# Loading the first weight matrix behind the row loads of the first batch, and stage 1 of the second batch one step later

## The chip, the cores and the metric

The kernel runs on one core of a Trainium2 chip. The metric is device time in microseconds (us) of one launch; each time given is the median of several runs. The engines are PE (matmuls; PEld is its weight loads), DVE and ACT (elementwise work and copies), POOL (a slower elementwise engine that also issues one of the two DMA queues) and SP (which issues the other). Each engine works through its own instructions in the order in which the program lists them, and waits on semaphores for the others and for DMAs.

## The reference

The input x has 8 batches of 3136 rows of 256 features. A filter is applied along the rows by an FFT, a product and an inverse FFT. Then a low-rank mix over the rows is added, and a two-layer MLP over the features with a residual:

```python
X = np.fft.rfft(x, axis=1)
y = np.fft.irfft(X * (filt_r + 1j * filt_i)[None], n=3136, axis=1)
h = y.transpose(0, 2, 1) @ U @ V              # rank 32
u = y + h.transpose(0, 2, 1)
out = u + np.maximum(u @ w_ch1, 0.0) @ w_ch2  # 256 -> 1024 -> 256
```

## The kernel before

3136 is 49 times 64, so each transform is done in two matmul stages. The work on one batch b goes through these generators, each of which issues a small piece and then yields:

- `f1(b)`, or `f1_turned(b)` for batches 0 and 1: stage 1. A batch of x is loaded by `load_x(b, c)` (L127) in four chunks c, with POOL issuing the DMA and the DMA casting to 16 bits. Stage 1 of a chunk is four pieces of four matmuls (L282, tile pf), each copied out of PSUM by a pair of copies on ACT or DVE (L288, L290, tile t).
- `mid(b)`: the second forward stage, the filter and the first inverse stage. For batches 0 and 1 `turn` transposes stage 1's result on PE (L308, tile pt) and copies it (L310, tile a), half on DVE and half on ACT. Then come matmuls (L383, tile pz), the product with the filter on DVE (L391, tile uv; L395 and L396 combine its halves) and matmuls again (L344, tile pe), which ACT copies to e (L354).
- `ct` and `eb`: each e is written to DRAM (tile ct, L363) and read back by `load_e2` (L415) in another order as rows of eb. A batch has three parts of 16, 16 and 12 rows of four, and each part is read in two halves, h = 0 (columns r below 32) and h = 1. Two last rows of frequencies of batch 0 go to eb directly (L358). SP issues ct and the reads of eb, in the order of the program.
- `rank(b)` writes the low-rank term into the first 32 rows of eb (L437, on DVE).
- `s4(b)`: the last inverse stage (L455, tile pu), whose result ut feeds the MLP.
- The MLP goes over 49 groups of 512 rows, eight steps for each group. A step does `mm1` (L487, weights w1sb, tile phh, a relu on ACT, L490) for its own group and `mm2` (L510, weights w2sb, tile pc; a residual, L502, on each second step) for the group before. DVE copies pc to och (L517), and POOL issues the store (L522).

Batch 0 runs through all of its stages ahead of the first step; `unread` issues matmuls that nothing reads. From then on `plan` holds, for each of the steps, which generators of the later batches move on by one piece behind that step's mm1 and mm2. `deal(gen, count, a, z)` spreads count pieces evenly over the steps a to z. In the first 48 steps batch 1 gets its stage 1 (the last twelve pieces, as four are done ahead), its mid, its rank and its s4.

The change touches two places. One is what POOL does between filters and steps. In its queue the program lists, one behind another: filters, V, constants, chunk 0 of batch 1, w1 (L553), copies of the filters, two direct rows of eb, and then this block:

```python
for h in range(2):
    for p in (32, 64):
        nc.gpsimd.tensor_copy(seen[p:p + 32], eb[p:p + 32, 8 + 32 * h, 0:4])
    for c in ((1,), (2, 3))[h]:
        load_x(1, c)
nc.gpsimd.dma_start(w2sb, ...)
```

Nothing uses `seen` (L580). The copies read one column of a half of eb, so that POOL waits until that half of the rows has landed, and the loads listed after them are issued after that. The other place is the two lines of the plan for mid and stage 1 of batch 1.

Of the kernel before, what the change touches and what calls it, by code (L numbers as in the profile page):

```python
# [79 lines left out]
def kernel(  # L80
# [11 lines left out]
    nc = tc.nc  # L92
# [22 lines left out]
    def dram(t, off, dims):  # L115
        return bass.AP(tensor=t, offset=off, ap=[list(d) for d in dims])
# [7 lines left out]
    def load_x(b, c):  # L124
        t = sb.tile([98, 8 * DM], F16, tag="x", bufs=4, name="x")
        for a, n in ((0, 96), (96, 2)) if b == 0 else ((0, 98),):
            nc.gpsimd.dma_start(t[a:a + n], dram(x.tensor, (b * SEQ + 8 * c + 32 * a) * DM, [[32 * DM, n], [1, 8 * DM]]))  # L127
        xt[b, c] = t
# [30 lines left out]
    def spread_filters(i):  # L159
        s = slice(PARTS[i], PARTS[i + 1])  # L160
        copies = ((nc.vector.tensor_copy, nc.scalar.copy), (nc.vector.tensor_copy, nc.scalar.copy),
                  (nc.gpsimd.tensor_copy, nc.gpsimd.tensor_copy))[i]

        for s in (slice(PARTS[2], 19), slice(19, NK)) if i == 2 else (s,):
            for f, copy in enumerate(copies):
                copy(fab[64:128, f, s, :], fab[0:64, f, s, :])
# [12 lines left out]
    w1sb = cst.tile([128, 2, NH], F16)  # L179
# [5 lines left out]
    eb = cst.tile([97, NR, DM], F16)  # L185
# [11 lines left out]
    seen = cst.tile([128, 4], F16)  # L197
# [42 lines left out]
    def f1(b):  # L240
        for c in range(4):
            t = xt[b, c].rearrange("p (j d) -> p j d", d=DM)
            asb = sb.tile([98, 8, DM], F16, tag="asb", bufs=4, name="asb")
            for half in range(2):
                for i in range(2):
                    pf = bank("z", "pf")
                    for s in range(2):
                        j = 4 * half + 2 * i + s
                        nc.tensor.matmul(pf[0:98, 256 * s:256 * s + 256],  # L249
                                         ws[:, (8 * c + j) * 98:(8 * c + j + 1) * 98], t[:, j, :],  # L250
                                         start=(s == 0), stop=True, skip_group_check=True)
                    dst = asb[:, 4 * half + 2 * i:4 * half + 2 * i + 2, :]
                    src = pf[0:98].rearrange("p (j d) -> p j d", d=DM)
                    nc.scalar.copy(dst, src)  # L254
                    if half and i:
                        nc.sync.dma_start(dram(ct1[b], 8 * c * 96 * DM, [[DM, 96], [96 * DM, 8], [1, DM]]), asb[0:96])
                        nc.sync.dma_start(dram(ct0[b], 8 * c * DM, [[32 * DM, 2], [1, 8 * DM]]),
                                          asb[96:98].rearrange("p j d -> p (j d)"))
                    yield
# [8 lines left out]
    def f1_turned(b):  # L268
        t1[b] = (sb.tile([128, 2, 24, 128], F16, tag="ut", bufs=2, name="t1"),
                 sb.tile([128, 2, NR], F16, tag="t10", bufs=1, name="t10"))  # L270
        for c in range(4):
            t = xt[b, c].rearrange("p (j d) -> p j d", d=DM)
            for n in range(4):
                half, dh = n // 2, n % 2
                pf = bank("z" if b else ("z", "m", "z", "o")[n], "pf")
                if b == 0:

                    unread(pf, 2 if (c, n) == (3, 0) else 0)
                    unread(pf, 1, 120)
                for s in range(4):  # L280
                    j = 4 * half + s
                    nc.tensor.matmul(pf[:, 98 * s:98 * s + 98], t[:, j, 128 * dh:128 * dh + 128],  # L282
                                     ws[:, (8 * c + j) * 98:(8 * c + j + 1) * 98],
                                     start=(s == 0), stop=True, skip_group_check=True)
                j = 8 * c + 4 * half

                copy = nc.vector.tensor_copy if dh and not (b and c < 1) else nc.scalar.copy
                copy(t1[b][0][:, dh, :, 4 * j:4 * j + 16].rearrange("p k (j c) -> p k j c", c=4),  # L288
                     view(pf, 0, [[1, 24], [98, 4], [24, 4]]))
                copy(view(t1[b][1], NR * dh + j, [[1, 4], [32, 2]]), view(pf, 96, [[98, 4], [1, 2]]))  # L290
                yield
# [236 lines left out]
    def deal(gen, count, a, z):  # L528
        for i in range(count):
            plan[max(0, int(a + i * (z - a) / count))].append(gen)  # L530

    def later_x(b, c):
        load_x(b, c)
        yield

    f1s = [f1(b) if b > 1 else f1_turned(b) for b in range(NB)]
    mids = [mid(0, "o")] + [mid(b) for b in range(1, NB)]
# [12 lines left out]
        next(f1s[0])  # L550
    nc.gpsimd.dma_start(sv[32:97], sv_d.rearrange("k (r q) -> k r q", q=NQ))
    load_x(1, 0)
    nc.gpsimd.dma_start(w1sb, moe_w_ch1.rearrange("(h dd) c -> dd h c", h=2))  # L553
    spread_filters(2)
    v_rows(nc.gpsimd.tensor_copy, 0, 32)
    for i in range(13):
# [18 lines left out]
            next(f1s[1])  # L575
        unread(pw, 1)

    for h in range(2):
        for p in (32, 64):
            nc.gpsimd.tensor_copy(seen[p:p + 32], eb[p:p + 32, 8 + 32 * h, 0:4])  # L580
        for c in ((1,), (2, 3))[h]:
            load_x(1, c)
    nc.gpsimd.dma_start(w2sb, moe_w_ch2.rearrange("(t cc) e -> cc t e", t=8))
    for _ in s4s[0]:
        pass
# [1 line left out]
    def loads(b, part):  # L587
        load_e2(b, part)
        yield

    for b in range(1, NB):
        a, z = S[b - 1], S[b]
        e = z - (17 if b == 1 else 20 if b < 6 else 22)
        deal(mids[b], 13, a + {1: 8, 2: -3}.get(b, -5), e - 4)
        deal(mids[b], 4, e - 4, e)
        for p, at in enumerate((e - 5, e - 4, e + 1)):
            plan[at].append(loads(b, p))
        deal(ranks[b], 6, e, e + 6)
        deal(s4s[b], 16, e + 8, z - 2)
        if b == 1:  # L600
            deal(f1s[1], 12, 1, 8)
        if b + 1 < NB:
            for c in range(4):
                plan[a + (9 + 2 * c if b == 1 else 1 + 4 * c)].append(later_x(b + 1, c))
            deal(f1s[b + 1], 16, a + (21 if b == 1 else 10), z - (13 if b == 1 else 20))
# [40 lines left out]
```

## Time and profile before

| | |
|---|---|
| median of 3 runs | 520.44 us (519.37 to 521.15) |
| the profiled execution: its own time | 522.24 us |
| its span, first to last instruction | 520.5 us |
| granted clock of PE, mean | 0.993 |
| busy: PE, DVE, ACT, POOL | 497.2, 352.3, 377.1, 80.7 us |
| moved by DMA | 88.22 MB |

Times in the profile are counted from the first instruction of the span. In a line of the timeline the columns are start, duration, engine, line, operation, out<-in, and in brackets the idle time before it and what ended that. A line of the chain gives start, duration and what it was. A window gives its bounds and length, busy time of the engines with the number of instructions, PE's granted clock, the share of the DMA engines' time that was busy, and GB/s. A landing is counted from the issue of the DMA.

### The profile page before, as it was taken

To read this page: it belongs to the slowest core of one execution; us is meant where nothing else is said; L and a number is where in the kernel's file an instruction comes from. 1 tells how busy PE (TensorE), PEld (TensorE's weight loads), DVE (VectorE), ACT (ScalarE), POOL (GpSimd) and SP (SyncE) were. 2 spreads that over 40 slices of the span, in tenths; PEclk is the share of its full clock that TensorE was granted. 3 is DMA by queue.
4 is the path that set the end of the run, shared out by engine and by line. 5 is a ranking of instruction groups with operands and counts; after the bars stand their busy time and mean duration, and the time that the engine had idled before them with its cause. 6 is when DMAs were issued, how large, how long until landed. Compare 5 with 4: busy or idle time off the path is not lost.

```text
span 520.5 us, 11966 instructions
## 1 busy us (share of the span) xinstructions
PE 497.2 (96%) x4852; PEld 355.4 (68%) x4852; DVE 352.3 (68%) x469; ACT 377.1 (72%) x704; POOL 80.7 (15%) x122
## 2 busy tenths in 40 slices
PE   4887899999999999999999999899999999999997
PEld 4545556776767776777767777577667766776665
DVE  5886698588847974788747974689745995621112
ACT  6875779767985789668976799467985677666662
POOL 6662010111010120111010110012010010101110
PEclk9998999999999999999999999899999999999999
DMA  8997846758685586828684597618875136212113
GB/s 194 179 216 175 151 110 188 234 198 171 181 265 206 117 222 207 273 87 185 180 275 180 130 236 218 239 42 196 235 232 199 62 134 189 107 42 83 81 42 122
DMA packets 67375, 88.22 MB, mean 170 GB/s; under 512 B 4835, under 2 KB 51875, under 8 KB 67320
## 3 DMA queue, kind: packets, MB, share of 16 engines
q0 software_dynamic: 14704, 41.58, 30.8%
q1 hardware_dynamic: 52616, 45.88, 28.8%
q8 instruction: 38, 0.62, 0.5%
q14 instruction: 17, 0.14, 0.1%
HBM read 55.20 MB, written 47.78 MB: 198 GB/s over the span
## 4 chain that ended last, share of the span: by engine, by line
PE 82%; DMA 8%; DVE 4%; ACT 2%; issue 1%; POOL 1%; SPq 0%; POOLq 0%; DVEq 0%; ACTq 0%
PE pc L510 31%; PE phh L487 30%; PE pu L455 5%; PE pc L502 4%; PE pf L249 4%; PE pe L344 4%; PE pz L383 3%; DVE uv L391 2%; DMA ct<-e 2%; DMA w2sb<-in_moe_w_ch_dram 2%; DMA x<-in_x_dram 2%; DMA eb<-ct 2%; PE ph L422 1%; DMA fab<-in_filt_i_dram 1%; POOL x L127 1%
## 5 line engine op out<-in xcount | busy, mean ns | idle before, releaser
L490 ACT ACTIVATE h<-phh 128x512 f16<-128x512 f32 x392 | 235.9, 603 | 90.3 <-PE phh L487 88.8
L510 PE MATMUL pc<-w2sb,h 128*128 128x256 f16 x1568 | 234.9, 273 | 0.4 <-DMA w2sb<-in_moe_w_ch_dram 0.4
L487 PE MATMUL phh<-ut,w1sb 128*128 128x512 f16 (+7 forms) x896 | 233.9, 353 | 0.4 <-DVE ut L462 0.4
L510 PEld LDWEIGHTS <-h 128*128 128x128 f16 x1568 | 151.7, 97 | 91.8 <-issue 1.5
L517 DVE COPY och<-pc 128x512 f32<-128x512 f32 x98 | 67.6, 690 | 99.5 <-PE pc L502 98.2
L391 DVE TENSOR_TENSOR uv<-pz,fab 128x1024 f16<-128x1024 f32 (+1 forms) x104 | 120.8, 1179 | 12.6 <-PE pz L383 10.4
L522 POOL DMA_DIRECT2D out_dram<-och x48 | 39.0, 813 | 408.2 <-DVE och L517 392.5
L487 PEld LDWEIGHTS <-w1sb 128*128 128x128 f16 x896 | 77.5, 97 | 19.2 <-issue 1.5
L354 ACT CAST e<-pe 128x512 f16<-128x512 f32 x96 | 56.5, 591 | 19.4 <-PE pe L344 18.8
L462 DVE CAST ut<-pu 128x392 f16<-128x392 f32 x92 | 48.8, 560 | 23.8 <-PE pu L455 22.2
L254 ACT CAST asb<-pf 98x512 f16<-98x512 f32 x96 | 57.2, 598 | 0.2
L502 PE MATMUL pc<-idn,ut 128*128 128x128 f16 (+1 forms) x400 | 54.2, 220 | 0.0
L437 DVE COPY eb<-h 32x4096 f16<-32x4096 f16 x32 | 38.2, 1232 | 14.2 <-ACT h L434 14.1
L455 PE MATMUL pu<-sv,eb 97*128 97x49 f16 x1024 | 40.8, 188 | 4.8 <-DMA eb<-ct 4.8
L344 PE MATMUL pe<-uv,m 128*128 128x512 f16 (+1 forms) x117 | 41.3, 371 | 2.4 <-DVE uv L391 1.3
L455 PEld LDWEIGHTS <-eb 97*128 97x128 f16 x1024 | 37.8, 98 | 6.2 <-DVE eb L437 3.1
L502 PEld LDWEIGHTS <-ut 128*128 128x128 f16 (+1 forms) x400 | 38.2, 98 | 5.4 <-issue 0.8
L383 PE MATMUL pz<-a,m 128*128 128x512 f16 x96 | 36.2, 379 | 1.1 <-DVE a L310 1.0
L249 PE MATMUL pf<-x,ws 98*98 98x256 f16 x192 | 36.7, 273 | 0.0
L395 DVE TENSOR_TENSOR uv<-uv 64x1024 f16<-64x1024 f16 (+1 forms) x49 | 30.9, 630 | 1.7
L396 DVE TENSOR_TENSOR uv<-uv 64x1024 f16<-64x1024 f16 (+1 forms) x49 | 30.8, 628 | 0.7
L249 PEld LDWEIGHTS <-ws 98*98 98x98 f16 x192 | 22.4, 125 | 9.1 <-issue 0.4
(78 smaller groups left out, 225.8 us busy)
## 6 DMA issues: line engine op xcount, KB each, us to landing
out_dram<-och POOLq DMA_DIRECT2D x48, 512.0 KB, 3.8
ct<-e SPq DMA_DIRECT2D x47, 256.0 KB
eb<-ct SPq DMA_DIRECT2D x46, 256.0 KB
x<-in_x_dram POOLq DMA_DIRECT2D x28, 392.0 KB, 7.8
ct<-asb SPq DMA_DIRECT2D x24, 384.0 KB
a<-ct SPq DMA_DIRECT2D x18, 512.0 KB
x<-in_x_dram POOLq DMA_DIRECT2D x4, 384.0 KB, 8.0
ws<-ws SPq DMA_DIRECT2D x1, 600.2 KB
```

The costliest lines, as they stand in the source:

```text
L249: nc.tensor.matmul(pf[0:98, 256 * s:256 * s + 256], ws[:, (8 * c + j) * 98:(8 * c + j + 1) * 98], t[:, j, :], start=(s == 0), stop=True, s ...
L254: nc.scalar.copy(dst, src)
L344: nc.tensor.matmul(pe[:, 0:n], w, uv[:, f, o:o + n], start=(f == 0), stop=(b > 0 or f == 1))
L354: nc.scalar.copy(t[:, 2 * (i % 2):2 * (i % 2) + 2, :].rearrange("p k d -> p (k d)"), pe)
L383: nc.tensor.matmul(pz, a2m, src[:, k:k + 2, :].rearrange("p k d -> p (k d)"), start=True, stop=True)
L391: nc.vector.tensor_mul(uv[:, :, o:o + n], zin, fin)
L455: nc.tensor.matmul(pu[:, NQ * i:NQ * i + NQ], eb[:, 8 * n + i, d], sv[:, 8 * g + i, :], start=(i == 0), stop=True, skip_group_check=True)
L487: nc.tensor.matmul(ph[:, o:o + n], w1sb[:, dh, 128 * t:128 * t + 128], utv(b)[:, dh, t0:t0 + n], start=(dh == 0), stop=(dh == 1), skip_gro ...
L490: nc.scalar.activation(h, ph, RELU)
L502: nc.tensor.matmul(d, w, idn, start=False, stop=(dh == 1), skip_group_check=True)
L510: nc.tensor.matmul(o, gr.h[tt][:, 128 * i:128 * i + 128], w2sb[:, tt, :], start=(tt == 0), stop=False, skip_group_check=True)
L517: nc.vector.tensor_copy(gr.och[:, i - 1:i + 1, :], gr.pc.rearrange("p (j d) -> p j d", d=DM))
```

## The change

w1 is no longer issued behind chunk 0 of batch 1. It is issued behind a new copy into seen of two rows, 32 and 33, at column 8; these belong to the first halves of parts 0 and 1. The other copies and the loads of chunks 1 to 3 and w2 keep their order and now follow w1. The twelve pieces of stage 1 of batch 1 are dealt over steps 2 to 9 in place of 1 to 8 (the bound at the end is left out), and mid of batch 1 starts at step 9 in place of 8; the step at which its thirteen pieces end stays.

```diff
     load_x(1, 0)
-    nc.gpsimd.dma_start(w1sb, moe_w_ch1.rearrange("(h dd) c -> dd h c", h=2))
     spread_filters(2)
...
-    for h in range(2):
-        for p in (32, 64):
-            nc.gpsimd.tensor_copy(seen[p:p + 32], eb[p:p + 32, 8 + 32 * h, 0:4])
-        for c in ((1,), (2, 3))[h]:
-            load_x(1, c)
+    for parts, r in ((((32, 34),), 8), (((32, 64), (64, 96)), 8), (((32, 64), (64, 96)), 40)):
+        for p, q in parts:
+            nc.gpsimd.tensor_copy(seen[p:q], eb[p:q, r, 0:4])
+        if len(parts) == 1:
+            nc.gpsimd.dma_start(w1sb, moe_w_ch1.rearrange("(h dd) c -> dd h c", h=2))
+        else:
+            for c in (1,) if r == 8 else (2, 3):
+                load_x(1, c)
     nc.gpsimd.dma_start(w2sb, moe_w_ch2.rearrange("(t cc) e -> cc t e", t=8))
...
-        deal(mids[b], 13, a + {1: 8, 2: -3}.get(b, -5), e - 4)
+        deal(mids[b], 13, a + {1: 9, 2: -3}.get(b, -5), e - 4)
...
-            deal(f1s[1], 12, 1, 8)
+            deal(f1s[1], 12, 2, 9)
```

## The prediction

> **What bounds the kernel now.** I read the page first (busy shares, chain), then the chain between 30 and 80 us, the SP queue and its waits, the windows of the DMA engines, and the timeline of PE and DVE.
>
> ```profile
> PE 497.2 (96%) x4852; PEld 355.4 (68%) x4852; DVE 352.3 (68%) x469; ACT 377.1 (72%) x704; POOL 80.7 (15%) x122
> PE 82%; DMA 8%; DVE 4%; ACT 2%; issue 1%; POOL 1%; SPq 0%; POOLq 0%; DVEq 0%; ACTq 0%
> ```
>
> PE fills the span, so a change here counts only by the time PE loses before the stretch from about 76 us on, where it is busy without a break (16.00 of 16.00 us in the window 76 to 92). The chain says who holds PE before that:
>
> ```profile
> 36.14 3.45 DMA ct<-e
> 41.98 3.88 DMA eb<-ct
> 47.65 10.36 DMA w2sb<-in_moe_w_ch_dram
> 59.13 0.70 DVE a L310
> 75.17 0.70 DVE a L310
> ```
>
> Three stretches: the rows of batch 0 (ct written, read back into eb), then loads up to w2 at 58.01, then DVE. The SP queue and its waits:
>
> ```profile
> 27.00 5.02 SPq L363 DMA_DIRECT2D ct<-e  x3
> 34.81 0.59 SPq L415 DMA_DIRECT2D eb<-ct  x1
> 39.65 3.13 SPq L415 DMA_DIRECT2D eb<-ct  x4
> SPq L415 <- DMA ct<-e: 3.8, 3, 1.9
> ```
>
> The first read of rows (34.81) waits for ct writes issued by 27.4, some 7 us before. A later write took 3.45 us (first line of the chain above). The early ones ran beside w1, whose entry is
>
> ```profile
> L553 POOL DMA_DIRECT2D w1sb<-in_moe_w_ch_dram x1: 1005/1005/1005, 20.6 to 20.6; - x1
> DMA to landing us min/median/max: 12.9/12.9/12.9
> ```
>
> so it was in flight from 20.6 to 33.5. This is what the change can win. The windows of the loads (the second last number is the share of the DMA engines):
>
> ```profile
> 45.00:58.00 13.00, 10.47 (x165) 7.41 (x162) 7.21 (x18) 10.41 (x27) 3.98 (x8) 0.92 1.00 165
> 40.00:45.00 5.00, 2.18 (x52) 1.97 (x51) 3.43 (x6) 0.97 (x2) 0.94 (x3) 0.87 0.68 202
> ```
>
> From 45 to 58 the DMA engines are full: x chunks 1 to 3 release PE at 50.50, 53.27 and 55.42, w2 at 58.05. From 40 to 45 a third of them is free. Last, PE and DVE after that:
>
> ```profile
> 58.05 0.60 PE L510 MATMUL pc<-w2sb,h 128*128 128x256 f16 x4 [0.42 <-DMA w2sb<-in_moe_w_ch_dram]
> 60.09 0.59 PE L487 MATMUL phh<-ut,w1sb 128*128 128x512 f16 x2
> 60.29 2.42 DVE L391 TENSOR_TENSOR uv<-pz,fab 128x1024 f16<-128x1024 f32 x2 [0.47 <-PE pz L383]
> 75.91 0.38 PE L383 MATMUL pz<-a,m 128*128 128x512 f16 x1 [0.70 <-DVE a L310]
> ```
>
> DVE starts on batch 1 at 59.13, right behind the transposes at 58.49, and from 60.29 to its copy that ends at 75.86 no gap is over 0.05 us; PE then waits 0.70 us for that copy. So from 58 to 76 the time is DVE's start plus a fixed 16.7 us of work.
>
> **Part 1: w1 leaves 20.64.** POOL loses an issue of 1.0 us there. It gains nothing by it: its next work, a filter copy at 23.68, waited 2.0 us for a DMA. x chunk 0 of batch 1 stands ahead of w1 in the same queue. DVE multiplies back to back from 21.5 to 34.6, so that stage does not shorten. What moves is SP. If the early ct writes land by 32, the first row read goes at 32.1, when SP is free, in place of 34.81. The two ct writes behind it then leave at their results (ACT ends them at 33.66 and 34.79), not at 35.5 and 36.1. The reads of the third part need the last of them: 34.83 + 3.45 = 38.3, or 37.5 if it lands faster (SP issues the two direct rows up to then: result at 36.21 plus 1.20). Today they start at 39.65. So the rows gain 1.3 to 2.1 us; at worst nothing, if the writes were slow for another reason. I take 1.7: PE starts on the rows at 41.3 rather than 43.06. Its clock was 0.50 from 44 to 47, behind the idle gap; with a gap of 1.1 us it may stay at 1.00. Neither helps by itself, as PE waits for x at 50.50 anyway.
>
> **Part 2: w1 comes back behind the first halves of parts 0 and 1.** POOL waits with a two-row copy (0.18 us), then issues w1 (1.0 us). Queued behind it are the other copies into seen, x chunks 1 to 3 and w2, and PE waits for all of these loads. POOL was idle from 37.6 to 42.97, so the instructions hide if it is released by 41. The read of part 1 would leave SP at 35.4 (36.67 today). The third read let POOL go 3.3 us after its issue (39.65 to 42.97), so w1's issue comes at 39 at the earliest and 42 if nothing gets faster; I take 39.5 to 40.5, and bytes from 41 on.
>
> Its cost on the DMA engines: w2, of the same 512 KB, took from 55.42 to 58.05, 2.6 us; x at its best 2.15 us for 392 KB, which makes 2.8. I take 2.6, its own size and kind. Today the engines' work from 40 to w2 is 5.0 x 0.68 + 13.0 x 1.00 = 16.4 us. Add 2.6; take off the row traffic that now falls ahead of 40, 1.7 x 0.65 = 1.1 (the share between 40 and 41); 17.9 is left. At a share of 0.7 until 41 and 1.0 after it w2 lands at 41 + 17.2 = 58.2, **0.2 us later**. The bounds are wide. If w1 takes on the slow start of the stream (chunk 1 needed 6.8 us from its issue, against 2.15 between later chunks) w2 could land up to 2.8 us earlier; there ACT is the floor (seven relus of 0.60 and five pairs of copies of 0.68 come before it: 7.6 us from 47.5, so 55.1). If w1 starts at 42 and nothing overlaps, it is 2.6 to 2.9 us later. I stay near the middle because the free share from 40 to 45 (5 x 0.32 = 1.6 us) and the earlier rows about pay for 2.6.
>
> The first use of w1, at 49.10 today, then comes at about 48; w1 lands between 46 and 48.5. A wait there is hidden as long as x and w2 are later, and they are.
>
> The Trainium skill speaks against this part: in "DMA: Bandwidth & Descriptors", section "Rules for kernel authors", it says to issue a DMA early and wait on its semaphore late. By it w1 at 20.64, landed 15 us ahead of its use, is free where it stands, and the sum would be the late rival below. The trace agrees with half of that: w1 made no one wait at its use, but SP waited 3.8 us for writes that ran beside it.
>
> **Part 3: stage 1 a step later.** The twelve pieces of f1 go from steps 1 to 7 to steps 2 to 8; they issue no DMA, only four matmuls and a pair of copies each. So mid of batch 1 starts at step 9. Its SP writes move with it; SP's queue is empty from 42.8 to 68.1, so nothing waits there. Today w2's arrival is followed by one mm2 (0.44 us) and the transposes. Afterwards it is followed by that mm2, the last f1 piece (0.35), mm1 of step 9 (0.43), its mm2 (0.44) and residual (0.11), and then the transposes. DVE starts **1.3 us later** against w2. The work between the first and the third copy of a on DVE is the same and in nearly the same order, so the 16.7 us stay. PE does more in between: it waits longer for DVE but has one step (0.87) more behind it, so at that point the loss is 0.4. But two steps on the matmul of L344 at 80.32 follows DVE's add at 80.26, and there the full 1.3 comes back. Bounds: 0.4 and 1.3; I take 1.3, as that row is a direct handover.
>
> **Sum.** +0.2 + 1.3 = +1.5 us. The profiled execution took 522.24 us, 520.5 span and 1.7 around it; the next would take 523.7. The runs' median is 520.44, 1.8 below the profiled one, so I forecast **521.9**. 0.3% is 1.56 us, about what a measurement of this kernel can tell from no change.
>
> **Rivals.**
> - *w1 late* (slower). If the rows come no sooner, w1 is issued at 42, and x and w2 queue behind 2.6 us more: w2 at 60.6 to 60.9, and with the 1.3 it makes +3.9 to +4.2; half of that delay +2.6. For it: 45 to 58 is full already, and the row reads also wait for results of ACT at 36.21. Against: 3.8 us of SP waits on ct. It decides when the two-row copy runs after 41. About 523.9; chance 0.20.
> - *w1 fits in, and DVE's step is absorbed* (faster). The slow start falls on w1, w2 lands at 55.2 at ACT's floor (-2.8), and only 0.4 of DVE's step is left: -2.4, 518.0. For it: the free third from 40 to 45, and rows up to 2.1 us early. Against: L344's direct handover. Chance 0.22.
> - *A draw.* The stream gains 1.3 us and DVE's step takes it: 520.4. Chance 0.13.
> - The forecast, +0.7 to +2.3: chance 0.45, of which 0.26 lies over 0.3%.
>
> Slower 0.20 + 0.26 = 0.46; same 0.19 + 0.13 = 0.32; faster 0.22. The range runs from inside the fast rival to the middle of the late one, 518.2 to 523.9, and leaves out about half of each.
>
> **What would show it.** The first row read at about 32, the four at 37.5 to 38.5, the two-row copy at 39 to 40.5: part 1 right. w2 releasing PE at 58.2: part 2. DVE's first copy at 60.6 and PE's wait for the third at about 77: part 3. A two-row copy after 41.5 is the late rival; w2 before 56.5, or DVE's start not 1.8 us or more behind it, the fast one.

## The result, and the profile after

The changed kernel took **520.9 us** (median of 22 runs, 518.87 to 524.03), the kernel before 519.5 beside it (22 runs, 517.31 to 524.22); the ratio is 1.0033, with a 95% interval of 1.0017 to 1.0049. That is 0.9 to 2.5 us slower. The forecast was 521.9, in a range of 518.2 to 523.9.

The first view of the profile after is the timeline of the SP queue, with the SP queue's waits below it (engine, line and what it waited for: sum in us, times, longest).

```profile
32.19 0.58 SPq L415 DMA_DIRECT2D eb<-ct  x1
33.76 1.49 SPq L363 DMA_DIRECT2D ct<-e  x2
37.54 2.98 SPq L415 DMA_DIRECT2D eb<-ct  x4
...
SPq L363 <- ACT e L354: 6.6, 5, 2.4
SPq L415 <- DVE uv L391: 0.3, 1, 0.3
```

The wait of the reads for ct (3.8 us before) is gone. The first row read leaves at 32.19 instead of 34.81 and the four reads at 37.54 instead of 39.65. POOL's timeline shows what is released by them:

```profile
39.97 0.22 POOL L580 COPY seen<-eb 2x4 f16<-2x4 f16 x1 [2.29 <-DMA eb<-ct]
40.47 0.95 POOL L582 DMA_DIRECT2D w1sb<-in_moe_w_ch_dram  x1 [0.29 <-issue]
42.67 0.59 POOL L127 DMA_DIRECT2D x<-in_x_dram  x1
45.16 1.09 POOL L127 DMA_DIRECT2D x<-in_x_dram  x2
46.42 0.92 POOL L586 DMA_DIRECT2D w2sb<-in_moe_w_ch_dram  x1 [0.17 <-issue]
```

Every issue of POOL behind the rows is now sooner than before, w2's by 1.2 us (47.65). All the same, what PE waits for ends later. These are the lines of its timeline with a DMA in the brackets:

```profile
41.23 0.36 PE L455 MATMUL pu<-sv,eb 97*128 97x49 f16 x8 [0.92 <-DMA eb<-ct]
44.55 0.36 PE L455 MATMUL pu<-sv,eb 97*128 97x49 f16 x8 [1.06 <-DMA eb<-ct]
49.93 2.74 PE L487 MATMUL phh<-ut,w1sb 128*128 128x512 f16 x6 [3.18 <-DMA w1sb<-in_moe_w_ch_dram]
58.83 0.60 PE L510 MATMUL pc<-w2sb,h 128*128 128x256 f16 x4 [1.11 <-DMA w2sb<-in_moe_w_ch_dram]
```

PE starts on the rows 1.8 us sooner and loses it again in a new wait of 3.18 us for w1, the largest in this stretch. The wait that counts is the last: w2, at 58.83 instead of 58.05. The windows of the loads (the second last number is the DMA share) show why it is later:

```profile
28.00:34.00 6.00, 5.41 (x24) 2.06 (x22) 6.00 (x6) 4.80 (x9) 4.35 (x3) 1.00 0.71 188
34.00:40.00 6.00, 5.08 (x57) 2.75 (x56) 4.33 (x4) 3.71 (x12) 1.15 (x3) 1.00 0.63 187
40.00:45.00 5.00, 3.02 (x92) 2.63 (x90) 4.38 (x8) 1.94 (x4) 3.19 (x7) 1.00 0.87 207
45.00:58.00 13.00, 9.54 (x123) 5.84 (x120) 5.37 (x14) 8.43 (x23) 3.70 (x7) 0.87 1.06 188
```

In before the last two shares were 0.68 and 1.00, and the first two stretches were:

```profile
28.00:34.00 6.00, 5.42 (x24) 2.07 (x22) 6.00 (x6) 4.80 (x9) 5.07 (x3) 1.00 1.03 243
34.00:40.00 6.00, 5.08 (x56) 2.75 (x56) 4.34 (x4) 3.71 (x12) 1.08 (x2) 1.00 0.73 195
```

(The share adds up the recorded times of packets, which overlap, so it can be above 1.) So w1 left the stretch from 28 to 34, where it delayed the rows, and went into the one that ends with w2. Part of the row traffic left that one. These are SP's queue from 40 to 60, before and after, in packets, MB and share of the 16 engines' time:

```profile
q1 hardware_dynamic: 431, 1.02, 16.9%
q1 hardware_dynamic: 250, 0.79, 12.2%
```

Of 20 us that is 3.4 us of work before and 2.4 after. Last, DVE's copies of a and, behind the third, the matmul of L344 that takes its next add:

```profile
61.07 0.69 DVE L310 COPY a<-pt 128x1024 f16<-128x1024 f16 x1 [0.77 <-PE pt L308]
62.23 2.35 DVE L391 TENSOR_TENSOR uv<-pz,fab 128x1024 f16<-128x1024 f32 x2 [0.47 <-PE pz L383]
...
77.16 0.69 DVE L310 COPY a<-pt 128x1024 f16<-128x1024 f16 x1
...
82.31 0.39 PE L344 MATMUL pe<-uv,m 128*128 128x512 f16 x1
```

The first copy is 1.94 us later than before (59.13), the third 1.99 (75.17), the matmul of L344 1.99 (80.32). From there the relus of the steps stand 1.98 to 2.00 us later, up to the one that begins at 214 us in before. This is the change's cost up to there. From 216 us on it is 2.29 us in this profile; no cause was sought for the last 0.3.

The spans of the two profiles say the opposite: 520.5 before, 519.2 after. The cause lies far behind the change. Before's profiled execution has this line in PE's timeline, and PE's clock was 0.50 for 3.4 us behind it:

```profile
333.10 0.59 PE L455 MATMUL pu<-sv,eb 97*128 97x49 f16 x16 [2.01 <-DMA eb<-ct]
```

A second profile of before (below) has no such wait and a span of 516.6, so it belongs to one execution, and the comparison goes by the runs' times and by the places up to 214 us.

### The profile page after: what moved, and what is told of

The parts are those of the page before. It is cut to its first block, busy times and chain, and to the rows that moved or that the text cites. A ratio compares the mean times of both kernels' runs of the same rounds, so it can differ in the third digit from the quotient of the medians.

```text
span 519.2 us, 11970 instructions
## 1 busy us (share of the span) xinstructions
PE 495.3 (95%) x4852; PEld 353.1 (68%) x4852; DVE 351.8 (68%) x469; ACT 377.1 (73%) x704; POOL 81.9 (16%) x123
## 4 chain that ended last, share of the span: by engine, by line
PE 82%; DMA 5%; DVE 5%; ACT 2%; SPq 1%; issue 1%; POOL 0%; POOLq 0%; ACTq 0%
PE pc L510 31%; PE phh L487 30%; PE pu L455 5%; PE pc L502 4%; PE pf L249 4%; PE pe L344 4%; PE pz L383 3%; DVE uv L391 3%; DMA w2sb<-in_moe_w_ch_dram 2%; DMA eb<-ct 2%; DMA ct<-e 1%; PE ph L422 1%; ACT e L354 1%; ACT h L490 1%; DVE och L517 1%
## 5 line engine op out<-in xcount | busy, mean ns | idle before, releaser
L462 DVE CAST ut<-pu 128x392 f16<-128x392 f32 x92 | 48.5, 558 | 18.7 <-PE pu L455 18.6
L344 PE MATMUL pe<-uv,m 128*128 128x512 f16 (+1 forms) x117 | 41.3, 371 | 3.2 <-DVE uv L391 2.2
L455 PE MATMUL pu<-sv,eb 97*128 97x49 f16 x1024 | 39.2, 185 | 2.2 <-DMA eb<-ct 2.0
L455 PEld LDWEIGHTS <-eb 97*128 97x128 f16 x1024 | 36.1, 96 | 3.9 <-issue 1.6
```

What stands on the lines that cost most here:

```text
L344: nc.tensor.matmul(pe[:, 0:n], w, uv[:, f, o:o + n], start=(f == 0), stop=(b > 0 or f == 1))
L455: nc.tensor.matmul(pu[:, NQ * i:NQ * i + NQ], eb[:, 8 * n + i, d], sv[:, 8 * g + i, :], start=(i == 0), stop=True, skip_group_check=True)
```

## The experiments

Each time is compared with runs of before on the same chip. In the expectations and below, "offset" is how much later than in before's profile (36.51) POOL issued the two direct rows in the profile named. It shows how much a profile was late for other reasons, and is only good to some tenths.

| kernel | us, before's | ratio and interval | offset | PE on rows | first use of w2 | first copy of a | third copy |
|---|---|---|---|---|---|---|---|
| before | | | 0 | 43.06 | 58.05 | 59.13 | 75.17 |
| before again | 518.34, one run | | 0.58 | 43.48 | 57.94 | 59.02 | 75.05 |
| after | 520.90, 519.50 | 1.0033 (1.0017 to 1.0049) | 0.06 | 41.23 | 58.83 | 61.07 | 77.16 |
| steps only | 520.06, 518.79 | 1.0019 (0.9997 to 1.0041) | 0.06 | 44.20 | 58.36 | 60.60 | 76.69 |
| w1 only | 520.25, 518.79 | 1.0025 (1.0005 to 1.0045) | 0.72 | 41.68 | 59.24 | 60.32 | 76.35 |
| no w1 | 517.24, 518.79 | 0.996 (0.994 to 0.998) | 0.78 | 42.23 | 56.71 | 57.79 | 73.82 |
| w1 behind V | 521.27, 518.79 | 1.0051 (1.0031 to 1.0071) | 0.53 | 44.38 | 60.73 | 61.82 | 77.85 |
| w1 in halves | 519.23, 519.22 | 0.999 (0.9972 to 1.0008) | 0.59 | 42.91 | 58.32 | 59.40 | 75.43 |
| w1 behind direct rows | 521.53, 519.22 | 1.003 (1.000 to 1.0059) | -0.06 | 40.90 | 58.22 | 59.30 | 75.34 |
| the same, w2 in halves | 520.83, 519.22 | 1.0028 (1.0002 to 1.0054) | 0.26 | 41.92 | 60.14 | 61.22 | 77.26 |
| transposes first | 519.30, 518.80 | 1.0002 (0.9981 to 1.0024) | 0.42 | 42.71 | 58.38 | 57.42 | 73.89 |
| halves, transposes first | 518.75, 518.80 | 1.0005 (0.9984 to 1.0025) | 0.35 | 42.35 | 60.06 | 59.10 | 75.56 |

The two profiles of before agree to 0.1 us at w2 and at the copies, although the rows are 0.4 us apart and the offset is 0.58. So an offset does not simply come off at w2.

**The steps only.** w1 stays at its old place.

```diff
-        deal(mids[b], 13, a + {1: 8, 2: -3}.get(b, -5), e - 4)
+        deal(mids[b], 13, a + {1: 9, 2: -3}.get(b, -5), e - 4)
-            deal(f1s[1], 12, 1, 8)
+            deal(f1s[1], 12, 2, 9)
```

> w1 where the kernel before has it; only the steps of f1 and mid of batch 1 one later. Theory (loads set w2's arrival, DVE's chain behind it sets the rest): w2 releases PE at 58.05 as before, DVE's first copy of a comes 2.2 us behind that instead of 1.1, its third copy at 76.3 (75.17 before, 77.16 after the change); +1.2 us, ratio 1.0023. Rival (the step is absorbed, all of the loss is w1's): third copy at 75.2 to 75.6, ratio 1.000.

Measured: +1.0 us (-0.2 to +2.1). The interval includes zero, so the size comes from the profile. The row to read is the distance from w2's matmuls to the first copy: 58.36 to 60.60 is 2.24 us, and it is 2.24 after as well, while it is 1.08 in both profiles of before. So the step costs 1.16 us and is not absorbed: the third copy follows the first by 16.09 us (16.04 before).

**w1 only.** The block on POOL is that of the change, the steps are those of before.

> w1 behind the first rows as in the change; the steps of f1 and mid of batch 1 as before. Theory: rows and w2 as in the change (rows on PE at 41.2, first mm1 waiting for w1 until 49.9, w2 at 58.8), DVE's first copy of a 1.1 us behind w2, third copy at 75.95; +0.8 us, ratio 1.0015. Rival (the later steps are needed to ride out the late chunks of x): PE waits for chunk 1 at 51.6 and loses more, w2's matmuls later than 59, third copy at 77 or later.

Measured: +1.3 us (+0.3 to +2.3). w2 is first used at 59.24, 1.08 us ahead of the first copy, as in before. PE's timeline:

```profile
50.10 1.04 PE L487 MATMUL phh<-ut,w1sb 128*128 128x512 f16 x4 [2.67 <-DMA w1sb<-in_moe_w_ch_dram]
52.10 0.84 PE L282 MATMUL pf<-ws,x 98*128 98x98 f16 x8 [0.96 <-DMA x<-in_x_dram]
58.81 0.59 PE L487 MATMUL phh<-ut,w1sb 128*128 128x512 f16 x2 [0.17 <-ACT h L490]
```

Here w2 landed at 59.05, while PE's own work ended at 59.24. So PE, held up by w1, by x, by a clock of 0.50 from 51.95 to 55.36 and at last by ACT, is 0.2 us later than the load: the wait for w1 is hidden, but with nothing to spare. Together the two halves make 2.3 us by the runs, more than the change's 1.7 but within the intervals.

**No w1.** w1 is not loaded; its tile is set to zero at the old place.

> w1 is not loaded at all: POOL fills w1sb with zeros at the place where the kernel before issues w1, so the MLP adds nothing; steps as before. Theory: the first read of rows leaves SP at 32.2 and the four at 37.5 as in the change, x chunk 1 is issued at 41.5 and lands at 48.2, w2 at 55.8, third copy of a at 72.9: -2.3 us, ratio 0.9957; so the earlier rows are worth 2.3 us and w1's place in the stream costs 3.0. Rival (w2 is not set by the stream but by ACT or by PE): PE reaches w2's matmuls without a wait for the DMA, at 56.5 or later, -1.5 us or less.

Measured: -2.1 us (-3.1 to -1.0) by the runs. By the profiles it is less: w2 is used 1.34 us sooner than in before (1.23 sooner than in before again), and the third copy stands 1.35 us sooner. PE waited 1.55 us for w2 here, so the rival, that ACT or PE sets its use, fell. This prices w1 at both places. At 20.64 it costs before 1.2 to 1.3 us by the rows of the profiles, by holding up the rows of batch 0. Behind them it costs more: w2 is first used at 58.83 after against 56.71 here, 2.1 us, or 2.8 with this run's offset (0.72 more than after's) taken off. The earlier rows and the load nearly cancel, and the load is the larger. That the runs gain more than the profiles has a possible second cause: PE's granted clock, the mean of the twelve runs, was 0.9995 here and 0.9957 in the runs of before beside them. Whether the missing load or the zeros in w1 made that difference was not tested.

**w1 behind V**, at 32.43, when POOL is free from the copies of V:

```diff
-    nc.gpsimd.dma_start(w1sb, ...)
     spread_filters(2)
     v_rows(nc.gpsimd.tensor_copy, 0, 32)
+    nc.gpsimd.dma_start(w1sb, ...)
```

> w1 issued by POOL right behind the last copy of V (about 33), ahead of the direct rows and of all waits for rows; steps as before. Theory: its bytes fall into the free share of the DMA engines between 34 and 40; the first read of rows at 32.2, but the last ct writes go beside w1, so the four reads come at 38.5 to 39.6; w2 at 57 to 57.7, third copy of a at 74.1 to 74.9, -0.3 to -1.0 us, ratio 0.998 to 0.9995. Rival (ct writes starve beside any 4 KB stream as they did before): four reads at 40.5 or later, w2 at 58.5 or later, ratio 1.001 or more.

Measured: +2.6 us (+1.6 to +3.7). My theory fell and the rival held: the four reads came at 40.94 and w2 was used at 60.73 (w1's packets in the trace are of 2 KB, not of the rival's 4). It was the slowest of all, and the SP queue says where:

```profile
32.67 0.60 SPq L415 DMA_DIRECT2D eb<-ct  x1
34.23 1.49 SPq L363 DMA_DIRECT2D ct<-e  x2
40.94 2.99 SPq L415 DMA_DIRECT2D eb<-ct  x4
...
SPq L415 <- DMA ct<-e: 2.7, 1, 2.7
```

The ct writes were issued within half a microsecond of after's, but landed at 40.0 to 40.9 (36.1 to 36.9 after), so that the last reads were 3.4 us later.

**w1 in halves of its columns**, one at the old place and one behind the two-row copy, with the steps of before.

> The steps are those of before. The first 512 columns of w1 (256 KB) are issued where before issues all of w1, the last 512 behind the two-row copy. If the cost at each place goes by the bytes, half of each is seen: the second part's ct writes are free about 3 us earlier than in before (half of w1's 12.9 us in flight), so the first row read goes at 32.2 to 33.5 and the rows reach PE at 41.3 to 42.3; half of the 2.8 us that w1 costs the stream comes back, 1.4, so that w2 lands at 57.0 to 58.0 (58.01 in before, 55.9 without any w1) and DVE's third copy of a stands at 74.6 to 75.6: -0.6 to +0.4 us against before. Rival: a half starves the small writes nearly as long as the whole (the packets are 1 KB for 2 KB, so there are as many turns): first row read at 34 or later, w2 at 59 or later, +0.6 us or more.

Measured: no difference (-1.5 to +0.4 us). The first row read left at 34.47, w2 was used at 58.32, and the third copy stood at 75.43: the time and the third copy lie where the theory by bytes put them, w2 is 0.3 us above its bound, and the first row read (33.5 at most by the theory, 34 or later by the rival) is where the rival had it. Half of w1 at the old place held the rows almost as the whole did; what the other half cost the stream fits its bytes. Neither theory is borne out whole, and the sum is nothing.

**w1 behind the two direct rows**, at 37.55, with no wait ahead of it; the same with w2 in two DMAs.

```diff
     next(mids[0])
+    nc.gpsimd.dma_start(w1sb, ...)
     v_rows(nc.vector.tensor_copy, 32, NR)
...
-    nc.gpsimd.dma_start(w2sb, ...)
+    for t in (0, 4):
+        nc.gpsimd.dma_start(w2sb[:, t:t + 4], ...)
```

> The steps are those of before; w1 is issued by POOL right behind the two direct rows' DMAs, at about 37.7, with no copy that waits for rows ahead of it, so some 2.8 us before the place that the change gives it (40.47). All ct writes of the first pass have landed by then (36.9 in the profile after). Theory (w1's price in the stream is what it takes beyond the free share of 36 to 45): the share at 38 to 40 was 0.46 in the profile after, which leaves 1.1 us of engine time free, so w2 lands 0.8 to 1.6 us before the w1-only kernel's 59.05 (offset of that run 0.72), at 56.5 to 57.8, the third copy of a at 73.7 to 75.0, and the time is -1.4 to -0.3 us against before. Rival: the row reads (64 KB in small packets) share turns with w1 as the ct writes did where w1 stood at 32.4; rows reach PE at 43 or later, the copies that let POOL issue x come late, w2 at 58.5 or later, 0 to +1.5 us.

> As the kernel with w1 behind the direct rows, and w2 in two DMAs of four tiles each (256 KB), since the first mm2 group needs only tiles 0 to 3. If w2's landing is what holds PE at step 8 there too, the first mm2 is free up to 1.3 us earlier (half of w2's 2.6 us), DVE's first copy stands 0.5 to 1.3 us earlier than in that kernel, and the time is another 0.4 to 1.2 us lower. Rival: the relus and pairs of copies that ACT owes between chunk 3 and w2 end no earlier (w2 found ACT and PE 0.4 to 1.1 us idle only in before and after), so that 0 to 0.4 us is gained.

Both theories fell: 2.3 and 1.6 us slower by the medians, where a gain was expected. PE's timeline with w1 behind the direct rows:

```profile
40.90 0.37 PE L455 MATMUL pu<-sv,eb 97*128 97x49 f16 x8 [0.72 <-DMA eb<-ct]
46.51 0.36 PE L455 MATMUL pu<-sv,eb 97*128 97x49 f16 x8 [3.35 <-DMA eb<-ct]
58.22 0.60 PE L510 MATMUL pc<-w2sb,h 128*128 128x256 f16 x4 [0.94 <-DMA w2sb<-in_moe_w_ch_dram]
```

The first half of the rows came early, as w1 is behind it. The second half shared with w1 and came at 46.51 (44.55 after); POOL's copy that waits for it let chunks 2 and 3 and w2 go only at 47.13 and 48.20, and the DMA engines then had free time between (a share of 0.22 from 47 to 48). The reads are 256 and 192 KB each, not the 64 KB of the expectation. In the run with w2 in halves the second half of the rows came at 48.70, a wait of 4.51 us, and PE, whose clock was 0.50 from 47.4 to 54.3, reached step 8 at 60.14, behind both halves of w2 (57.79, 59.20). So whether a smaller first half of w2 helps was not tested by it. The profile of the first of the two was that kernel's fastest run of twelve (518.62, with a median of 521.53), so its rows show the mechanism but not the usual size.

**Before again.**

> The kernel before, profiled once more, unchanged. If the 2.0 us wait of PE for rows of batch 5 at 333.1 and the clock of 0.50 behind it belong to that one execution and not to the kernel, no wait over 1 us stands there now and the span is 517.5 to 519, 1.5 to 3 us below the 520.5 of the profile before. If it belongs to the kernel, wait and half clock come again, and the change would be what takes them away.

Measured: span 516.6, own time 518.34, no wait over 0.4 us in batch 5. The span is a little below what was expected.

**The transposes first.** In before DVE's first copy stands behind the mm2 that waits for w2 by order alone. Here step 8 runs the plan's pieces ahead of its mm2.

```diff
-            if n:
+            if n and (n, t) != (1, 0):
                 mm2(groups[n - 1], t)
             for gen in plan[8 * n + t]:
                 next(gen, None)
+            if (n, t) == (1, 0):
+                mm2(groups[0], 0)
```

> Before's places for w1 and its steps; only in step 8 the first piece of mid of batch 1 (the transposes and DVE's first copy of a) is issued ahead of the step's mm2. In before the transposes stand behind mm2, which waits 0.42 us for w2 and takes 0.44 us. Theory (DVE's start sets the end of this stretch, and it is behind w2 by order alone): the transposes start at 57.5 to 58.0 in place of 58.49, w2 is used behind them with no wait, the first copy stands at 58.2 to 58.7 (59.13), the third at 74.3 to 74.8 (75.17), and the time is 0.4 to 0.9 us lower. Rival: the last pair of copies of stage 1 in ACT's queue ends only as w2 lands, so the transposes wait for ACT instead, first copy at 58.9 or later and 0 to 0.2 us gained.

> The same order in step 8, with w1 in halves of columns, one in before's place and one behind the two-row copy. With w2 out of DVE's way, chunk 3 of x sets its start; in the kernel with the halves alone it landed at 55.65 in a run whose direct rows stood 0.59 us later than in before, so 0.3 us sooner. If both effects add, the third copy stands another 0.2 to 0.4 us sooner than with the order alone (offset taken off), and the time is 0.6 to 1.3 us below before's. Rival: stage 1 and ACT, not x, hold the transposes; then the halves bring nothing on top.

The order did what it should. PE's timeline of the first:

```profile
56.44 0.22 PE L308 MATMUL pt<-idn,t 128*128 128x128 f16 x1
56.82 1.01 PE L308 MATMUL pt<-idn,t 128*128 128x128 f16 x15 [0.16 <-DVE t L288]
58.38 0.60 PE L510 MATMUL pc<-w2sb,h 128*128 128x256 f16 x4
```

w2 is used with no wait. From the release of chunk 3 (54.39) to the first copy (57.42) it is 3.03 us, where before takes 3.71 (55.42 to 59.13): 0.68 gained. But the first copy to the third takes 16.47 us (16.04), so 0.25 is left, below what the runs tell: 1.0002 and, with the halves, 1.0005. (The third copy stands 1.28 us sooner than in before, 73.89 for 75.17, but 1.03 of that is chunk 3, which came sooner in this execution with the loads where before has them.) In the second run the same distances are 3.03 and 16.46, and chunk 3 released PE at 56.07; so the halves bring x no sooner. None of the kernels that load w1 is faster than before by an interval that excludes zero.

**The clock in the runs.** The clock is a rival that none of these kernels tests. Among the 31 runs of before beside the first kernels, the twelve with a mean granted clock of 0.993 or less have a median of 519.95 us and the seven at 1.000 one of 518.03; those between follow no clear order. For the change this explains nothing, as after's mean is 0.9958 and before's lies at 0.9956 to 0.9969 wherever it was listed. But it was 0.9923 and 0.9926 in the two kernels with w1 behind the direct rows (0.9956 in before beside them), and 0.9944 and 0.9943 in the two with the transposes first (0.9969). So part of what their runs show against their profiles may be the clock.

## Why the prediction was right, and where it was not

**Part 1 held in every row.** The first row read was put at 32.1 (32.19), the four at 37.5 to 38.3 (37.54), PE on rows at 41.3 (41.23). That it is worth nothing by itself was true of this kernel, where PE then waited 3.18 us for w1. It is not true in general: in the kernel without w1 the earlier rows let POOL issue the loads sooner, and w2 was used 1.34 us sooner.

**Part 2 had the mechanism right and its net size too small:** +0.2 for w2, measured +0.78. By the windows the work from 40 to w2 is 5 x 0.87 + 13 x 1.06 + about 0.8 = 18.9 us, that is 16.4 + 2.5, where 16.4 + 1.5 was forecast. The term of the row traffic "that now falls ahead of 40" held: 1.1 us was taken off, and SP's queue has 0.9 us less behind 40 (3.4 and 2.4 above).

The term that failed is w1's 2.6. As a delay of w2 it was near what the kernel without w1 shows (2.1 to 2.8). But it is the time between two landings, and the 16.4 that it was added to is a sum of packet times. In the packet records of the traces w1's 256 packets of 2 KB took 3.5 us of the 16 engines' time in after and 3.3 in the kernel with w1 only, and w2's own 1024 packets of 512 B took 4.0 in before. The other parts nearly cancel: the packets of chunks 1 to 3 took 0.8 us less than in before (about 0.33 us each for 0.38), those of w2 0.2 less, and 0.9 us more of the next batch's x ran ahead of w2's last packets.

At the forecast's shares 18.9 us of work would have put w2 at 59.2. That it came at 58.83 is due to the stretch from 45 on, which ran at 1.06 instead of 1.00; the one from 40 to 45 held less than taken (4.35 us for 4.7).

w1's landing was missed: 46 to 48.5 forecast, 49.88 measured. Its first packets ran at 42.4, not 41, and from 46 on it shared with chunk 1, which had been issued 2.2 us behind it. The claim that a wait there is hidden held, because x and w2 came later, but by less than assumed: the kernel with w1 only shows PE and w2 level.

**Part 3 was right:** 1.3 forecast, 1.16 measured (the distance of 2.24 against 1.08), and 16.09 us from the first copy to the third (16.04 before), so that nothing was absorbed there. The handover at L344 took the whole delay on, 80.32 to 82.31. One sign failed as named. PE has no wait at the third copy any more, as a step more of its work lies there; it waits for DVE a moment earlier instead, 0.74 us at 75.76, and again for 0.84 us at 80.89.

**The sum** was +1.5. The rows give 0.78 + 1.16 = 1.94, the third copy 1.99, the runs 1.4 by the medians and 1.7 by the ratio. The forecast in us lies 1.0 above the result because it starts from 520.44; before ran at 519.5 beside the change.

**The rivals.** "w1 late" needed a two-row copy after 41; it came at 39.97. "Fits in, and DVE's step is absorbed" needed w2 near 55.2 and a third copy that keeps its distance to w2; the kernel without any w1 has w2 at 56.71 (55.9 with the offset off), so not even a free w1 would have given that, and the kernel with the steps only shows the step in full. The draw needed 1.3 us gained on the stream; with w1 only, the stream lost.

**The page that spoke against it.** The Trainium skill, "DMA: Bandwidth & Descriptors", section "Rules for kernel authors", advises to issue a DMA early and wait late. The runs agree in sign: w1 alone at the later place is 1.3 us slower. They also show what the rule leaves out, that the early issue was not free: without w1 the kernel is 2.1 us faster by the runs and 1.3 by w2's use.

**PE's clock** was 1.00 on the rows, as "may stay" had it. But a stretch at 0.50 came at the end of the wait for w1, from 49.2 to 52.6. Ahead of the span's end such stretches are 3.4 or 6.8 us long in all profiles here. In before the first begins at 43.7, in its second profile at 44.8, and three kernels (no w1, w1 in halves, transposes first) have none. The Trainium skill, "TensorE: Matmul & The Clock Gate", section "What's actually happening", describes a free-running window of about 3.4 us, so that the phase decides; the lengths and the shifting places agree.

## What to carry to other kernels

Before a load is moved, ask which stage bounds the transfers: a load taken out of a stage where it only delays others gains nothing if it goes into a full stream that ends the next wait. When such a stream is added up, keep all terms in one measure: here 2.6 us between two landings was added to a sum of packet times, in which the load took 3.5. And count a delayed step from the event that releases it to the handover that takes it on; here a step later was 1.16 us on the path, whatever else ran beside it.

## What the runs showed of the hardware that was not expected

In one run a stream on one DMA queue held short transfers on the other for longer than its own share of the turns, as they stood in order behind a read that it slowed. With w1 behind V the packet records of the trace show SP's first row read (64 packets of 4 KB) running from 34.5 to 38.0 beside w1's packets of 2 KB, about 12 against 16 in each half microsecond. The same read ran from 33.5 to 35.3 after. The ct writes, packets of 512 B that take 0.027 us each, stand behind that read on the same queue and began only behind 38.5. The Trainium skill, "DMA: Bandwidth & Descriptors", section "Queues, rings and completion order", says that a DMA engine takes turns between its queues packet by packet and consumes one queue's ring in order; turns near one for one and writes that wait for the read agree with that. That the order within the queue, not the turns, is the larger part was read from the records of one run, and was not tried by a kernel of its own.
